# Router logits summed on VectorE from the output rows in some full slots of a two-layer mixture of experts

## The chip, the cores and the metric

The kernel runs on one core of one Trainium2 chip. The metric is the device time of one execution in microseconds (us). Before the change it is 702.29 us, the median of three runs (701.58 to 703.89).

## The reference, cut to what matters

A decayed linear attention (4 batches, 8 heads, 768 positions, head size 64) gives 3072 rows of 512. Two mixture-of-experts layers follow. The second layer's router reads the rows that the first layer gives out.

```python
def _moe_ref(x, modality_id, w_gate, modality_bias, w1, w2):     # layer 1
    logits = x @ w_gate + modality_bias[modality_id]
    e_idx = np.argmax(logits, axis=1)
    ...
    for e in range(E):
        h = np.maximum(x[mask] @ w1[e], 0.0)
        out[mask] = gate_w[mask, None] * (h @ w2[e])

def _moe2_ref(x, w_skip, w_gate, w1, w2):                        # layer 2
    skip_score = x @ w_skip
    do_compute = skip_score > 0
    xc = x[do_compute]
    logits = xc @ w_gate
    e_idx = np.argmax(logits, axis=1)
    ...
    out[do_compute] = xc + y
```

N = 3072 rows, D = 512, E = 8 experts, F = 1024, all fp32. For layer 2 every row of layer 1's output therefore needs nine dot products of length 512: eight columns of `w_gate` and one `w_skip`.

## The kernel before, in words

The attention comes first, and layer 1's router with it. It writes the rows to DRAM, and tables that tell which rows each expert gets. Then both layers work in **slots** of up to 256 rows of one expert. Layer 1 has up to 19 slots, layer 2 up to 20; how many there are, which expert each has, whether its weights are new and whether it has more than 128 rows (`full`) is computed on VectorE by `table` into the row of whole numbers `ei` (lines 208 to 278), and read into registers by `flag` (L318), `reg` (L315) and `is_full` (L324). All branches are taken at run time on these registers, on each engine by itself.

Matrix products are made in fp32r with a high and a low part of each operand, so each product is three matmuls. A full slot does this on TensorE, in this order (`slot`, from L850 on):

- `layer1` (L702): eight column tiles f of 128, twelve matmuls each, 256 columns moving, into the PSUM tiles `p1`. After each odd f ScalarE takes the high part `hh` (L718) and VectorE the low part `hl` (L719) of the hidden rows.
- `trans_x` (L347): eight transposes of the next slot's gathered rows `xg`; ScalarE copies the high part `xth`, VectorE takes the low part `xtl` (L355).
- `layer2` (L748) for rows 0 to 127 and then for rows 128 to 255: eight chunks of three matmuls, 512 columns moving. The third matmul of a chunk takes `hl`: chunks 0 to 3 those of f = 1 and 3, chunks 4 and 5 that of f = 5, chunks 6 and 7 that of f = 7. ScalarE scales the result into `x2r` (L762), which is stored to DRAM (`keep`) and scattered to the output.

A slot kk of layer 1 also carries layer 2's **router for the rows of slot kk-1** (`router`, L661), as steps between the column tiles:

```python
steps = {1: lambda: tr(kk - 1, ptr), 3: la, 4: rk}
```

`tr` (L668) transposes the 256 rows `x2r` on TensorE, eight transposes, and ScalarE copies them to `x2t` (L669); `la` (L675) makes the logits, sixteen matmuls of 32 rows into `plg`; `rk` transposes these on VectorE (L680) to `L` and makes mask, maximum, one-hot rows and counts (L682 to L685 and `route_a`, `route_s`, L115 to L133). `rb` then stands in `layer2` after chunk 3: two small matmuls of ranks (L137, L138), seven short operations on VectorE that end with the reciprocal (L158), and two scatters of the tables' rows on GpSimd.

Where a slot begins another expert, `split_w2` (L308) and `split_w1` (L302) split the new weights into high and low parts on ScalarE and VectorE. Slots that are not full take `layer1_half`. The order on each engine is the order of the code (a manual schedule); each engine waits on semaphores.

Of the kernel before, what the change touches and what calls it, by code (L numbers as in the profile page):

```python
# [9 lines left out]
F32 = mybir.dt.float32  # L10
# [8 lines left out]
P = 128  # L19
E = 8  # L20
# [14 lines left out]
@with_exitstack  # L35
def body(ctx: ExitStack, tc: tile.TileContext, qkv, cpk, w1, w2, out, dbg=None):
    nc = tc.nc
# [141 lines left out]
    def count(dst):  # L179
        n = rt.tile([P, E], F32, tag="t_n", name="t_n")  # L180
        nc.vector.tensor_tensor(out=n, in0=dst, in1=erow0, op=ALU.subtract)
        return n
# [5 lines left out]
    def choose(which, n):  # L188
        t = rt.tile([P, E], F32, tag="t_p", name="t_p")
        g = rt.tile([P, E], F32, tag="t_g", name="t_g")  # L190
        mx = rt.tile([P, 1], F32, tag="t_mx", name="t_mx")
        mp = rt.tile([P, 1], F32, tag="t_mp", name="t_mp")
# [12 lines left out]
        nc.vector.tensor_scalar(out=erow, in0=eid, scalar1=float(TP), scalar2=None, op0=ALU.mult)  # L205
        nc.vector.tensor_tensor(out=perm, in0=bc(eid.unsqueeze(2), [P, E, E]), in1=bc(ivec.unsqueeze(1), [P, E, E]), op=ALU.is_equal)

    def table(which):
        n = count(pcnt[which])
        x = rt.tile([P, KT, E], F32, tag="t_x", name="t_x")  # L210
        nr = rt.tile([P, E], F32, tag="t_nr", name="t_nr")
# [13 lines left out]
        nc.vector.tensor_copy(out=ei_[:, 4 * KT:4 * KT + 1], in_=cc[:, E:E + 1])  # L225
        ge = rt.tile([P, KT, E], F32, tag="t_ge", name="t_ge")
        nc.vector.tensor_tensor(out=ge, in0=bc(kvec.unsqueeze(2), [P, KT, E]), in1=bc(c1.unsqueeze(1), [P, KT, E]), op=ALU.is_ge)
        h = rt.tile([P, KT, E], F32, tag="t_h", name="t_h")
        nc.vector.tensor_tensor(out=h, in0=bc(kvec.unsqueeze(2), [P, KT, E]), in1=bc(cc[:, 0:E].unsqueeze(1), [P, KT, E]), op=ALU.is_ge)
# [5 lines left out]

        u = rt.tile([P, E], F32, tag="t_u", name="t_u")
        y = rt.tile([P, KT], F32, tag="t_y", name="t_y")
        base = rt.tile([P, KT], F32, tag="t_b", name="t_b")
        nc.vector.scalar_tensor_tensor(out=u, in0=cc[:, 0:E], scalar=-float(T), in1=erow, op0=ALU.mult, op1=ALU.add)
# [5 lines left out]
        pick(eid, y)  # L245
        nx = rt.tile([P, E, E], F32, tag="t_nx", name="t_nx")
        nc.vector.tensor_tensor(out=nx, in0=bc(c1.unsqueeze(2), [P, E, E]), in1=bc(c1.unsqueeze(1), [P, E, E]), op=ALU.is_ge)
        nxe = rt.tile([P, E], F32, tag="t_nxe", name="t_nxe")
        nc.vector.tensor_reduce(out=nxe, in_=nx, axis=AX.X, op=ALU.add)
        w = rt.tile([P, KT], F32, tag="t_w", name="t_w")  # L250
        hx = rt.tile([P, KT], F32, tag="t_hx", name="t_hx")
        g2 = rt.tile([P, E], F32, tag="t_g2", name="t_g2")
        g3 = rt.tile([P, E], F32, tag="t_g3", name="t_g3")
        nc.vector.tensor_scalar(out=g2, in0=nxe, scalar1=estar, scalar2=None, op0=ALU.add)
# [5 lines left out]
        fin = ge[:, :, E - 1]  # L260
        nw = rt.tile([P, KT - 1], F32, tag="t_nw", name="t_nw")
        if which:
# [10 lines left out]
        nc.vector.scalar_tensor_tensor(out=u, in0=cc[:, 0:E], scalar=float(T), in1=nr, op0=ALU.mult, op1=ALU.add)  # L273
        rem = rt.tile([P, KT], F32, tag="t_r", name="t_r")
# [48 lines left out]
    def is_full(ap):  # L323
        return nc.values_load(ap, engines=FE, min_val=0, max_val=1,  # L324
                              skip_runtime_bounds_check_because="it is a comparison's result")

# [335 lines left out]
    def router(ix, kk=None):  # L662
# [14 lines left out]

        def rk():
            L = rt.tile([P, 2, 32], F32, tag="L2", name="L2")
            nc.vector.transpose(out=L.rearrange("p j e -> p (j e)"), in_=plg)  # L680
            idf = rt.tile([P, 2], F32, tag="idf", name="idf")
# [19 lines left out]

        return tr, la, rk, rb  # L702

    def layer1(kk, steps):
        xh, xl = xth[kk % 2], xtl[kk % 2]
        for f in range(8):
            pt = p1[(f // 2) % 3]
# [14 lines left out]

    def layer1_half(kk, steps):
        fs_ = [steps[f] for f in sorted(steps)]
        xh, xl = xth[kk % 2], xtl[kk % 2]
        for g in range(2):
            o = p1[g].rearrange("p a t -> p (a t)")
            fs = slice(g * 512, (g + 1) * 512)
            for c in range(4):
                nc.tensor.matmul(o, xh[:, c, 0:P], w1h[c][:, fs], start=(c == 0), stop=False)  # L730
                nc.tensor.matmul(o, xl[:, c, 0:P], w1h[c][:, fs], start=False, stop=False)
                nc.tensor.matmul(o, xh[:, c, 0:P], w1l[c][:, fs], start=False, stop=(c == 3))
            nc.scalar.activation(out=hrow[g], in_=o.rearrange("p (a f) -> p a f", f=P), func=AF.Relu)
            if g < len(fs_):
                fs_[g]()
        for g in range(2):
# [4 lines left out]
            for a in range(2):  # L741
                as_ = slice(2 * a, 2 * a + 2)
                nc.vector.tensor_tensor(out=hl[g][:, as_, 0:P], in0=pt[:, as_], in1=f32(hh[g][:, as_, 0:P]), op=ALU.subtract)  # L743
        for st_ in fs_[2:]:
            st_()
# [31 lines left out]
    def first1():  # L777
# [26 lines left out]
        behind(ld_w1(e), got)  # L804
        ld_w2(e)
        gather_x(0, 2)
        fill()
# [5 lines left out]
    def first2():  # L813
        la, rk, rb = router(itl)[1:]

# [28 lines left out]
    def slots(which):  # L844
# [10 lines left out]
        def slot(kk, fl, full):  # L855
# [22 lines left out]
            if which == 0:  # L878
                tr, la, rk, rb = router(it[(kk - 1) % 6], kk - 1)
# [48 lines left out]

_INS = ["qkv", "cpk", "w1", "w2"]
_OUTS = [((3072, 512), "float32")]  # L930
# [50 lines left out]
```

## Time and profile before

| | |
|---|---|
| median of 3 runs (range) | 702.29 us (701.58 to 703.89) |
| profiled execution | 703.4 us |
| its span, first to last instruction | 701.7 us |
| busy: TensorE matmuls, weight loads | 671.0 us (96%), 596.9 us (85%) |
| busy: VectorE, ScalarE, GpSimd | 361.2 us (51%), 262.5 us (37%), 218.3 us (31%) |
| mean granted TensorE clock | 0.994 |
| moved by DMA | 109.67 MB, mean 156 GB/s |

The profile names engines PE (TensorE's matmuls), PEld (its weight loads), DVE (VectorE), ACT (ScalarE), POOL (GpSimd) and SP (the queue that issues most DMAs); a q behind the name means the engine's sequencer (register loads, branches, waits), which is not counted as busy. Busy times are shares of the whole span; attention, layer 1 and layer 2 follow one another in it, and what an engine's time is worth differs from one to the next. An engine's idle time costs nothing where another engine is the one waited for.

### The profile page before, as it was taken

The numbers are of one execution on the slowest core, as the hardware profiler recorded it, in microseconds if no ns is written. First come the engines' busy times: TensorE is split into PE (matmuls) and PEld (weight loads), VectorE is DVE, ScalarE is ACT, GpSimd is POOL, SyncE is SP. The second block draws the span as 40 slices with busy tenths as digits, with TensorE's granted clock in tenths as the row PEclk, the third lists the DMA queues.
The fourth block names the chain that finished last, engine by engine and source line by source line (L and its number), as shares of the span: only waits on it lengthen the run. The fifth ranks groups of instructions, "written<-read, shape, count | busy, mean of one in ns | idle before, by whom it ended". The sixth has DMA issues, their size and how long they took to land. (4 is left out here: it accounts for less than half of the span.)

```text
span 701.7 us, 16337 instructions
## 1 busy us (share of the span) xinstructions
PE 671.0 (96%) x5628; PEld 596.9 (85%) x5628; DVE 361.2 (51%) x924; ACT 262.5 (37%) x462; POOL 218.3 (31%) x287
## 2 busy tenths in 40 slices
PE   6999999899999999999999998988999999999993
PEld 5889988878988998789889987876998899887992
DVE  5656676763213315853133337858227575758650
ACT  2444434522221225822222227432116544556530
POOL 4356556343231132531311324323121112113121
PEclk9999999999999999999999999999999999999997
DMA  8778766747330133883201211722815558658500
GB/s 279 227 199 236 211 200 211 212 134 273 109 116 32 64 121 101 284 308 123 91 31 38 92 48 53 250 87 53 295 60 177 194 199 277 198 189 266 179 6 29
DMA packets 60505, 109.67 MB, mean 156 GB/s; under 512 B 18656, under 2 KB 18784, under 8 KB 60368
## 3 DMA queue, kind: packets, MB, share of 16 engines
q1 hardware_dynamic: 48400, 86.65, 38.4%
q0 software_dynamic: 9744, 20.47, 8.6%
q8 instruction: 61, 1.00, 0.6%
q10 hardware_dynamic: 2224, 0.93, 0.6%
q14 instruction: 76, 0.62, 0.3%
HBM read 84.08 MB, written 30.06 MB: 163 GB/s over the span
## 5 line engine op out<-in xcount | busy, mean ns | idle before, releaser
L711 PE MATMUL p<-xth,w1h 128*128 128x256 f32 x672 | 190.4, 283 | 6.3 <-ACTq L893 1.9
L712 PE MATMUL p<-xtl,w1h 128*128 128x256 f32 x672 | 187.3, 279 | 0.0
L713 PE MATMUL p<-xth,w1l 128*128 128x256 f32 x672 | 187.3, 279 | 0.0
L719 DVE SCALAR_TENSOR_TENSOR hl<-p,hh 128x512 fp32r<-128x512 f32 x84 | 57.7, 690 | 180.6 <-ACT hh L718 173.1
L752 PE MATMUL p<-w2h,hh 128*128 128x512 f32 x360 | 144.2, 401 | 0.0
L753 PE MATMUL p<-w2l,hh 128*128 128x512 f32 x360 | 141.3, 393 | 0.9 <-DVE w2l L312 0.8
L754 PE MATMUL p<-w2h,hl 128*128 128x512 f32 x360 | 141.5, 393 | 0.6 <-DVE hl L743 0.6
L711 PEld LDWEIGHTS p<-xth,w1h 128*128 128x128 f32 x672 | 126.2, 188 | 10.0 <-ACTq L893 2.4
L713 PEld LDWEIGHTS p<-xth,w1l 128*128 128x128 f32 x672 | 127.2, 189 | 0.1
L712 PEld LDWEIGHTS p<-xtl,w1h 128*128 128x128 f32 x672 | 126.4, 188 | 0.8 <-DVEq L772 0.2
L718 ACT ACTIVATE hh<-p 128x512 fp32r<-128x512 f32 x84 | 50.2, 598 | 183.4 <-PE p L713 181.0
L161 POOL DMA_INDIRECT out_dram<-x2r,it x43 | 46.5, 1081 | 204.1 <-DVE x2r L765 101.6
L754 PEld LDWEIGHTS p<-w2h,hl 128*128 128x128 f32 x360 | 67.6, 188 | 16.5 <-DVE hl L743 1.5
L753 PEld LDWEIGHTS p<-w2l,hh 128*128 128x128 f32 x360 | 67.7, 188 | 15.9 <-DVE w2l L312 2.6
L752 PEld LDWEIGHTS p<-w2h,hh 128*128 128x128 f32 x360 | 67.7, 188 | 13.1
L161 POOL DMA_INDIRECT tab<-pk,rows x28 | 31.9, 1140 | 143.4 <-issue 119.9
L165 POOL DMA_INDIRECT xg<-xs,it x54 | 60.1, 1112 | 30.8 <-issue 12.7
L312 DVE TENSOR_TENSOR w2l<-raw,w2h 128x1024 fp32r<-128x1024 f32 x48 | 55.9, 1219 | 7.6 <-ACT w2h L311 7.3
L311 ACT CAST w2h<-raw 128x1024 fp32r<-128x1024 f32 x48 | 49.1, 1048 | 23.6 <-issue 12.5
L762 ACT ACTIVATE x2r<-p,it 128x512 f32<-128x512 f32 x26 | 17.9, 688 | 106.8 <-PE p L754 97.1
L306 DVE TENSOR_TENSOR w1l<-raw,w1h 128x512 fp32r<-128x512 f32 x88 | 53.9, 682 | 0.8 <-ACT w1h L305 0.3
L305 ACT CAST w1h<-raw 128x512 fp32r<-128x512 f32 x88 | 47.0, 635 | 0.0
(215 smaller groups left out, 799.0 us busy)
## 6 DMA issues: line engine op xcount, KB each, us to landing
raw<-in_w_dram SPq DMA_DIRECT2D x96, 512.0 KB, 6.4
kq<-in_qkv_dram SPq DMA_DIRECT2D x48, 256.0 KB, 3.4
xs<-x2r SPq DMA_DIRECT2D x28, 256.0 KB, 2.6
v<-in_qkv_dram SPq DMA_DIRECT2D x24, 256.0 KB, 3.8
xs<-xr SPq DMA_DIRECT2D x24, 256.0 KB, 5.5
xs<-xgm SPq DMA_DIRECT2D x7, 512.0 KB
xg<-xs,it POOLq DMA_INDIRECT x54, 4.3
tab<-tini ACTq DMA_DIRECT2D x2, 416.0 KB
```

The costliest lines, as they stand in the source:

```text
L161: nc.gpsimd.indirect_dma_start(out=dst, out_offset=bass.IndirectOffsetOnAxis(ap=idx, axis=0), in_=rows, in_offset=None, bounds_check=dst.s ...
L165: return nc.gpsimd.indirect_dma_start(out=rows, out_offset=None, in_=src, in_offset=bass.IndirectOffsetOnAxis(ap=idx, axis=0), bounds_chec ...
L306: nc.vector.tensor_tensor(out=w1l[c][:, s], in0=raw1[:, c, s], in1=f32(w1h[c][:, s]), op=ALU.subtract)
L312: nc.vector.tensor_tensor(out=w2l[c], in0=r, in1=f32(w2h[c]), op=ALU.subtract)
L711: nc.tensor.matmul(o, w1h[c][:, fs], xh[:, c, :], start=(c == 0), stop=False)
L712: nc.tensor.matmul(o, w1h[c][:, fs], xl[:, c, :], start=False, stop=False)
L713: nc.tensor.matmul(o, w1l[c][:, fs], xh[:, c, :], start=False, stop=(c == 3))
L718: nc.scalar.activation(out=a, in_=pt, func=AF.Relu)
L719: nc.vector.scalar_tensor_tensor(out=b, in0=pt, scalar=0.0, in1=f32(a), op0=ALU.max, op1=ALU.subtract)
L752: nc.tensor.matmul(p2[j], a, w2h[g][:, i], start=(n == 0), stop=False)
L753: nc.tensor.matmul(p2[j], a, w2l[g][:, i], start=False, stop=False)
L754: nc.tensor.matmul(p2[j], b, w2h[g][:, i], start=False, stop=(n == 7))
```

## The change

A new input `wgr` holds the nine columns of the router's weights as nine rows of 512. One DMA in `first1` copies them to all 128 partitions (`wgb`). In slots 2 to 10 of layer 1 the logits of the preceding slot's rows can be computed on VectorE: for each of two halves of 128 rows and each of nine columns, one operation multiplies 512 elements of `x2r` with `wgb` and sums them into one element of `L` per partition (`lg`). `tr`, `la` and the VectorE transpose in `rk` are then left out.

Which slots do so is decided by the flag that said `full`. For layer 1 it now is 0 for up to 128 rows, 1 for a full slot, and 2 for a full slot whose predecessor and successor have the same expert. The slot's first layer is cut in three parts with a branch each: f = 0 and 1; f = 2 and 3 with the router, in three arms (flag 2: `lg`; flag 1: as before; flag 0: half); f = 4 to 7. Temporaries of `table`, `choose` and `rk` get one buffer each in place of two.

```diff
+    wgb = hp.tile([P, E + 1, D], F32, name="wgb")
...
-        nc.vector.tensor_scalar(out=ei_[:, 3 * KT:4 * KT], in0=rem, scalar1=float(P), scalar2=None, op0=ALU.is_gt)
+        if which:
+            nc.vector.tensor_scalar(out=ei_[:, 3 * KT:4 * KT], in0=rem, scalar1=float(P), scalar2=None, op0=ALU.is_gt)
+        else:
+            nc.vector.tensor_tensor(out=w[:, 0:KT - 2], in0=nw[:, 0:KT - 2], in1=nw[:, 1:KT - 1], op=ALU.max)
+            nc.vector.tensor_scalar(out=w[:, 0:KT - 2], in0=w[:, 0:KT - 2], scalar1=-1.0, scalar2=2.0, op0=ALU.mult, op1=ALU.add)
+            nc.vector.scalar_tensor_tensor(out=ei_[:, 3 * KT + 1:4 * KT - 1], in0=rem[:, 1:KT - 1], scalar=float(P),
+                                           in1=w[:, 0:KT - 2], op0=ALU.is_gt, op1=ALU.mult)
...
+        def lg(j, es):
+            for e in es:
+                nc.vector.tensor_tensor_reduce(
+                    out=x2t[:, :, j], in0=x2r[kk % 2][j].rearrange("p (c t) -> p c t", t=P),
+                    in1=wgb[:, e].rearrange("p (c t) -> p c t", t=P), scale=1.0, scalar=0.0, op0=ALU.mult, op1=ALU.add,
+                    accum_out=box["L"][:, j, e:e + 1])
...
         ld_w2(e)
+        nc.sync.dma_start(out=wgb, in_=bc(wgr.unsqueeze(0), [P, E + 1, D]))
         gather_x(0, 2)
...
-            with tc.If(full > 0, preferred_fallthrough_block=True) as c:
-                layer1(kk, steps)
-            with c.Else():
-                layer1_half(kk, {} if which else {1: steps[1], 3: lambda: (la(), rk())})
+            if which == 0 and 2 <= kk <= 10:
+                box["L"] = rt.tile([P, 2, 32], F32, tag="L2", name="L2", bufs=1)
+                own = nc.values_load(ei[0][0:1, 3 * KT + kk:3 * KT + kk + 1], engines=(ET.DVE,), min_val=0, max_val=2,
...
+                with tc.If(own > 1):
+                    lg(0, range(E + 1))
+                with tc.If(full > 0, preferred_fallthrough_block=True) as c:
+                    layer1(kk, {}, (0, 1))
+                with c.Else():
+                    half_rows(kk, 0)
+                with tc.If(full > 1, preferred_fallthrough_block=True) as c:
+                    lg(1, range(0, 4))
+                    layer1(kk, {}, (2, 3))
+                    lg(1, range(4, E + 1))
+                    rk(True)
+                with c.Else():
+                    with tc.If(full > 0, preferred_fallthrough_block=True) as c2:
+                        steps[1]()
+                        layer1(kk, {}, (2, 3))
+                        la()
+                        rk()
+                    with c2.Else():
+                        steps[1]()
+                        half_rows(kk, 1)
+                        la()
+                        rk()
+                with tc.If(full > 0, preferred_fallthrough_block=True) as c:
+                    layer1(kk, {}, range(4, 8))
+                with c.Else():
+                    half_cols()
+            else:
...
```

`layer1_half` is cut into `half_rows` and `half_cols` with the same operations; the other slots keep the old code.

The change moves instructions at three places.

TensorE, slot 2, from the last matmul of f = 1 to the first of f = 2. `ptr` are the PSUM tiles of the transposes, `p_1876` and `p_1879` those of f = 0, 1 and f = 2, 3. Before:

```order
L713 MATMUL p_1876<-xth_164,w1l_145 128x256
L668 MATMUL ptr_1877<-ident,x2r_1872 128x128 [waits Activation_49]
L668 MATMUL ptr_1877<-ident,x2r_1872 128x128 x3
L668 MATMUL ptr_1878<-ident,x2r_1873 128x128 [waits Activation_49,Pool_49]
L668 MATMUL ptr_1878<-ident,x2r_1873 128x128 x3
L711 MATMUL p_1879<-xth_164,w1h_138 128x256
```

Now (the first two rows are the end of the arm for slots that are not full, which the branch L918 follows):

```order
L747 MATMUL p_1877<-w1l_145,xth_164 128x512 [waits DVE_49]
L914 UNCONDITIONAL_BRANCH
L918 COMPARE_AND_BRANCH
L728 MATMUL p_1880<-xth_164,w1h_138 128x256
L729 MATMUL p_1880<-xtl_166,w1h_138 128x256
L730 MATMUL p_1880<-xth_164,w1l_142 128x256
```

The transposes stand in front of f = 2 no longer, and neither do the logits' products in front of f = 4; a branch stands there.

VectorE, slot 2, from the register loads on. Before (`hl` is the hidden rows' low part, `pmi` the PSUM tile of the logits):

```order
L318 TENSOR_LOAD ei_168
L324 TENSOR_LOAD ei_168
L884 COMPARE_AND_BRANCH
L719 SCALAR_TENSOR_TENSOR hl_1866<-p_1876,hh_1864 128x512 [waits Activation_49]
L719 SCALAR_TENSOR_TENSOR hl_1866<-p_1879,hh_1864 128x512 [waits Activation_49]
L680 STREAM_TRANSPOSE L_2881<-pmi 128x64 [waits PE_49]
L682 CAST idf<-it_159 128x2 [waits DMAHW4_49]
```

Now:

```order
L324 TENSOR_LOAD ei_168
L330 TENSOR_LOAD ei_168
L910 TENSOR_LOAD ei_168
L912 COMPARE_AND_BRANCH
L687 ISA x2t,L_2794<-x2r_1872,wgb 128x4x128 [waits DMAHW7_49,Activation_49]
L687 ISA L_2794 128x1
L687 ISA x2t,L_2794<-x2r_1872,wgb 128x4x128 [waits DVE_49]
```

Each sum is two instructions, the sum and the readout of its result. Nine such pairs stand ahead of `hl` of f = 1, four between `hl` of f = 1 and of f = 3, five between `hl` of f = 3 and the ranking, which `hl` of f = 5 follows. Each sum after the first waits for the readout in front of it.

SP, in `first1`, behind the loads of the second expert's weights (`raw`). Now:

```order
L296 DMA raw_137<-in_w_dram 128x2x512 [waits DMAHW6_49,DVE_49]
L829 DMA wgb<-in_wgr_dram 128x4608 [waits DMAHW7_49,PE_49,Pool_49]
L792 DMA xs_63<-x2r_1870 128x512 [waits DMAHW0_49,Activation_49]
L324 TENSOR_LOAD ei_168
L795 COMPARE_AND_BRANCH
```

The copy of the table stands between the weights and the first store of rows; before, that store came directly behind the weights.

## Rows read from the trace of the kernel before

**Rows 1.** The page, busy us (share of the span) and instructions of each engine.

```profile
PE 671.0 (96%) x5628; PEld 596.9 (85%) x5628; DVE 361.2 (51%) x924; ACT 262.5 (37%) x462; POOL 218.3 (31%) x287
```

**Rows 2.** Stretches: length, busy us of each engine (instructions), granted clock, DMA share, GB/s.

```profile
202.90:227.62 24.72, 24.72 (x195) 22.32 (x194) 6.83 (x26) 5.81 (x11) 6.44 (x9) 1.00 0.25 84
...
561.02:583.80 22.78, 22.78 (x153) 20.80 (x152) 14.63 (x20) 11.72 (x18) 4.41 (x4) 1.00 0.65 219
```

**Rows 3.** Timeline of PE, slot 3: start, us, engine, line, operation, tiles, shape, count.

```profile
205.52 0.28 PE L713 MATMUL p<-xth,w1l 128*128 128x256 f32 x1
205.64 1.04 PE L668 MATMUL ptr<-ident,x2r 128*128 128x128 f32 x8
...
210.24 0.28 PE L712 MATMUL p<-xtl,w1h 128*128 128x256 f32 x1
```

**Rows 4.** Timeline of PE, later in the same slot.

```profile
215.47 0.28 PE L713 MATMUL p<-xth,w1l 128*128 128x256 f32 x1
215.58 1.04 PE L351 MATMUL ptr<-ident,xg 128*128 128x128 f32 x8
...
219.22 0.18 PE L137 MATMUL pmi<-oh,tri 128*128 128x16 bf16 x1
...
219.83 0.39 PE L754 MATMUL p<-w2h,hl 128*128 128x512 f32 x1
...
227.39 0.40 PE L754 MATMUL p<-w2h,hl 128*128 128x512 f32 x1
227.62 0.28 PE L711 MATMUL p<-xth,w1h 128*128 128x256 f32 x1
```

**Rows 5.** Timeline of DVE, the same slot; in brackets idle time before, and who ended it.

```profile
206.52 0.69 DVE L719 SCALAR_TENSOR_TENSOR hl<-p,hh 128x512 fp32r<-128x512 f32 x1 [10.58 <-ACT hh L718]
...
210.94 0.13 DVE L682 CAST idf<-it 128x2 f32<-128x2 int32 x1
...
212.41 0.17 DVE L127 TENSOR_TENSOR oh<-oh,mk 128x16 bf16<-128x16 bf16 x1
212.62 0.36 DVE L133 TENSOR_TENSOR rs<-rs,oh 128x8 bf16<-128x8 bf16 x2
...
216.41 0.69 DVE L719 SCALAR_TENSOR_TENSOR hl<-p,hh 128x512 fp32r<-128x512 f32 x1 [1.97 <-ACT hh L718]
217.02 1.27 DVE L355 TENSOR_TENSOR xtl<-ptr,xth 128x512 fp32r<-128x512 f32 x2
219.46 0.17 DVE L141 COPY rs<-rs 128x8 bf16<-128x8 bf16 x1 [1.16 <-PE pmi L138]
...
220.56 0.17 DVE L158 RECIPROCAL pk<-s 128x2 f32<-128x2 f32 x1
```

**Rows 6.** Timeline of ACT, the same slot: the first half of the output rows.

```profile
222.32 0.69 ACT L762 ACTIVATE x2r<-p,it 128x512 f32<-128x512 f32 x1 [4.87 <-PE p L754]
```

**Rows 7.** DVE: a timeline row of eight; then groups by form, busy us, mean ns.

```profile
270.33 4.91 DVE L306 TENSOR_TENSOR w1l<-raw,w1h 128x512 fp32r<-128x512 f32 x8
...
L122 DVE SCALAR_TENSOR_TENSOR sc<-dd,pri 128x16 f32<-128x16 f32 x14 | 2.5, 175 | 0.5
L685 DVE SCALAR_TENSOR_TENSOR mk<-L,pres 128x2 f32<-128x2 f32 x14 | 2.3, 161 | 0.5
L233 DVE TENSOR_TENSOR t_x<-t_h,t_nxe 128x192 f32<-128x192 f32 x2 | 0.7, 358 | 0.1
L234 DVE TENSOR_REDUCE t_w<-t_x 128x24 f32<-128x192 f32 x2 | 0.7, 352 | 0.1
L198 DVE TENSOR_SCALAR eb<-estar 128x1 int32<-128x1 f32 x4 | 0.6, 154 | 0.1
```

**Rows 8.** DVE's sequencer, 220 to 223: ns min/median/max, first and last start.

```profile
L324 DVEq TENSOR_LOAD <-ei x1: 304/304/304, 222.2 to 222.2; - x1
...
L884 DVEq COMPARE_BRANCH  x1: 50/50/50, 222.6 to 222.6; - x1
```

**Rows 9.** DMA from 150 to 175 in 40 slices of 0.625 us, all queues.

```profile
GB/s 249 157 164 203 118 249 354 354 321 367 308 203 269 374 413 419 400 400 406 400 393 387 390 387 380 413 393 416 423 384 226 107 47 0 0 0 0 2 1 324
```

More of the change, by code (lines that the diff above doesn't have):

```diff
@@ L35, in body @@
 @with_exitstack
-def body(ctx: ExitStack, tc: tile.TileContext, qkv, cpk, w1, w2, out, dbg=None):
+def body(ctx: ExitStack, tc: tile.TileContext, qkv, cpk, w1, w2, wgr, out, dbg=None):
     nc = tc.nc
@@ L188, in choose @@
     def choose(which, n):
[L189 to L192, printed above, removed]
+        t = rt.tile([P, E], F32, tag="t_p", name="t_p", bufs=1)
+        g = rt.tile([P, E], F32, tag="t_g", name="t_g", bufs=1)
+        mx = rt.tile([P, 1], F32, tag="t_mx", name="t_mx", bufs=1)
+        mp = rt.tile([P, 1], F32, tag="t_mp", name="t_mp", bufs=1)
         b = eb[:, which]
@@ L245, in table @@
         pick(eid, y)
-        nx = rt.tile([P, E, E], F32, tag="t_nx", name="t_nx")
+        nx = rt.tile([P, E, E], F32, tag="t_nx", name="t_nx", bufs=1)
         nc.vector.tensor_tensor(out=nx, in0=bc(c1.unsqueeze(2), [P, E, E]), in1=bc(c1.unsqueeze(1), [P, E, E]), op=ALU.is_ge)
-        nxe = rt.tile([P, E], F32, tag="t_nxe", name="t_nxe")
+        nxe = rt.tile([P, E], F32, tag="t_nxe", name="t_nxe", bufs=1)
         nc.vector.tensor_reduce(out=nxe, in_=nx, axis=AX.X, op=ALU.add)
[L250 to L253, printed above, removed]
+        w = rt.tile([P, KT], F32, tag="t_w", name="t_w", bufs=1)
+        hx = rt.tile([P, KT], F32, tag="t_hx", name="t_hx", bufs=1)
+        g2 = rt.tile([P, E], F32, tag="t_g2", name="t_g2", bufs=1)
+        g3 = rt.tile([P, E], F32, tag="t_g3", name="t_g3", bufs=1)
         nc.vector.tensor_scalar(out=g2, in0=nxe, scalar1=estar, scalar2=None, op0=ALU.add)
@@ L260, in table @@
         fin = ge[:, :, E - 1]
-        nw = rt.tile([P, KT - 1], F32, tag="t_nw", name="t_nw")
+        nw = rt.tile([P, KT - 1], F32, tag="t_nw", name="t_nw", bufs=1)
         if which:
@@ L323, in is_full @@
     def is_full(ap):
-        return nc.values_load(ap, engines=FE, min_val=0, max_val=1,
-                              skip_runtime_bounds_check_because="it is a comparison's result")
+        return nc.values_load(ap, engines=FE, min_val=0, max_val=2,
+                              skip_runtime_bounds_check_because="it comes from comparisons' results")
     def XG(which, kk):
@@ L676, in la, with rk @@
                                      start=(c == 0), stop=(c == 3))
-        def rk():
-            L = rt.tile([P, 2, 32], F32, tag="L2", name="L2")
-            nc.vector.transpose(out=L.rearrange("p j e -> p (j e)"), in_=plg)
+        def lg(j, es):
[4 more added lines that the diff above has]
+                    accum_out=box["L"][:, j, e:e + 1])
+        def rk(have=False):
+            L = box.get("L")
+            if L is None:
+                L = rt.tile([P, 2, 32], F32, tag="L2", name="L2", bufs=1)
+            if not have:
+                nc.vector.transpose(out=L.rearrange("p j e -> p (j e)"), in_=plg)
             idf = rt.tile([P, 2], F32, tag="idf", name="idf")
@@ L700, in rb, with layer1 @@
                 scatter(tabv[1][j], pk[:, j, :], rows[:, j:j + 1])
-        return tr, la, rk, rb
-    def layer1(kk, steps):
+        return tr, la, rk, rb, lg
+    def layer1(kk, steps, fr=range(8)):
         xh, xl = xth[kk % 2], xtl[kk % 2]
-        for f in range(8):
+        for f in fr:
             pt = p1[(f // 2) % 3]
@@ L721, in layer1, with half_rows, half_cols @@
                 steps[f]()
-    def layer1_half(kk, steps):
-        fs_ = [steps[f] for f in sorted(steps)]
+    def half_rows(kk, g):
         xh, xl = xth[kk % 2], xtl[kk % 2]
[L726 to L735, printed above, removed]
+        o = p1[g].rearrange("p a t -> p (a t)")
+        fs = slice(g * 512, (g + 1) * 512)
+        for c in range(4):
+            nc.tensor.matmul(o, xh[:, c, 0:P], w1h[c][:, fs], start=(c == 0), stop=False)
+            nc.tensor.matmul(o, xl[:, c, 0:P], w1h[c][:, fs], start=False, stop=False)
+            nc.tensor.matmul(o, xh[:, c, 0:P], w1l[c][:, fs], start=False, stop=(c == 3))
+        nc.scalar.activation(out=hrow[g], in_=o.rearrange("p (a f) -> p a f", f=P), func=AF.Relu)
+    def half_cols():
         for g in range(2):
@@ L743, in layer1_half @@
                 nc.vector.tensor_tensor(out=hl[g][:, as_, 0:P], in0=pt[:, as_], in1=f32(hh[g][:, as_, 0:P]), op=ALU.subtract)
+    def layer1_half(kk, steps):
+        fs_ = [steps[f] for f in sorted(steps)]
+        for g in range(2):
+            half_rows(kk, g)
+            if g < len(fs_):
+                fs_[g]()
+        half_cols()
         for st_ in fs_[2:]:
@@ L813, in first2 @@
     def first2():
-        la, rk, rb = router(itl)[1:]
+        la, rk, rb = router(itl)[1:4]
         def arm(l1, js):
@@ L878, in slot @@
             if which == 0:
-                tr, la, rk, rb = router(it[(kk - 1) % 6], kk - 1)
+                tr, la, rk, rb, lg = router(it[(kk - 1) % 6], kk - 1)
                 steps = {1: lambda: tr(kk - 1, ptr), 3: la, 4: rk}
@@ L882, in slot @@
             full2 = is_full(ei[which][0:1, 3 * KT + kk + 1:3 * KT + kk + 2])
-            with tc.If(full > 0, preferred_fallthrough_block=True) as c:
-                layer1(kk, steps)
-            with c.Else():
-                layer1_half(kk, {} if which else {1: steps[1], 3: lambda: (la(), rk())})
+            if which == 0 and 2 <= kk <= 10:
+                box["L"] = rt.tile([P, 2, 32], F32, tag="L2", name="L2", bufs=1)
+                own = nc.values_load(ei[0][0:1, 3 * KT + kk:3 * KT + kk + 1], engines=(ET.DVE,), min_val=0, max_val=2,
+                                     skip_runtime_bounds_check_because="it comes from comparisons' results")
+                with tc.If(own > 1):
[23 more added lines that the diff above has]
+                with c.Else():
+                    half_cols()
+            else:
+                with tc.If(full > 0, preferred_fallthrough_block=True) as c:
+                    layer1(kk, steps)
+                with c.Else():
+                    layer1_half(kk, {} if which else {1: steps[1], 3: lambda: (la(), rk())})
+            box.pop("L", None)
             trans_x(which, kk + 1, ptr)
@@ L926, in body @@
         dbg(nc, locals())
-_INS = ["qkv", "cpk", "w1", "w2"]
+_INS = ["qkv", "cpk", "w1", "w2", "wgr"]
 _OUTS = [((3072, 512), "float32")]
@@ L963 @@
         _np.ascontiguousarray(ids).view(_np.float32)], axis=1)
+    inputs["wgr"] = _np.concatenate([_np.asarray(inputs[n]).reshape(hd, -1) for n in ("moe2_w_gate", "moe2_w_skip")], axis=1).T
     inputs["w1"] = _np.concatenate([inputs["moe_w1"], inputs["moe2_w1"]], axis=0)
```

24 lines of the change are left out of this document (12 added, 12 removed).

## The prediction

> **What bounds the kernel now.** I read the page's busy times first, then a table of stretches, then the timelines of one slot, engine by engine. TensorE is busy for 96% of the span [rows 1], so a change pays by what it takes out of TensorE's stream, unless it makes TensorE wait. The slot from 202.90 to 227.62 is a full slot of layer 1 with the router in it. [...]
>
> **Where it acts.** The reference's inputs send 1494, 6, 1319 and 253 rows to four experts in layer 1, which makes slots 0 to 5, 6, 7 to 12 and 13; 6 and 12 have 128 rows or fewer. The flag is 2 where the slots on both sides have the same expert, and the new code stands in slots 2 to 10 alone: it runs in 2, 3, 4, 8, 9 and 10. Slots 5, 6 and 7 keep the old steps in the other arms. So: six slots, in two runs of three.
>
> **What it removes.** In the slot shown, the last matmul of f=1 starts at 205.52 and the second of f=4 at 210.24: 4.72 us for 26 steps of the stream, with eight transposes between [rows 3] and the logits' products. From 210.24 to the last of f=7 at 215.47 there are 46 steps in 5.23 us [rows 3, 4], 0.114 us each. Without the router the 26 steps take 2.96 us: **1.76 us saved a slot, 10.6 us in six.** [...] The slot would be 24.72 - 1.76 = 22.96 us. Two ScalarE copies a slot go too; nobody waits for them but the removed products.
>
> **What it adds on VectorE.** Eighteen sums a slot, each a product of 128x512 fp32 with a running sum, and behind each a readout of one element; the next sum waits for that readout. No row shows the pair, so I build its pitch p. Eight subtractions of 128x512 fp32, both inputs in SBUF, with no wait between them take 4.91 us [rows 7]; with 0.69 for the last, a step is (4.91 - 0.69)/7 = 0.60. Reducing costs nothing extra: 192 elements take 352 ns reduced, 358 multiplied [rows 7]. A one-element operation takes 154 ns [rows 7]. From an end to the start of an operation that waits for it is 0.04 us (212.41 + 0.17, then 212.62 [rows 5]). **p = 0.60 + 0.15 + 0.04 = 0.79.** Below, 0.73: only the write of the sum counts (0.69 + 0.04). Above, 0.92: the readout starts only when the sum is written (0.69 + 0.04 + 0.15 + 0.04). I take 0.79, because independent operations do overlap by 0.09 in that row and the readout waits on nothing.
>
> [...]
>
> **Does VectorE keep up?** Times from the slot's start. The first nine sums need the first half of the last slot's rows, written at 222.32 + 0.69, which is 4.61 before the next start at 227.62 [rows 4, 6]. Nine sums are 7.1 us, so they end at 2.5, before hl of f=1 at h = 206.52 - 202.90 = 3.62 [rows 5]. Then come two hl at a step of 0.61 (216.41 to 217.02), nine sums, the ranking (210.94 to 212.62 + 0.36: 2.04) and hl of f=5 (0.69). That hl is written at h + 1.22 + 9p + 2.73. TensorE needs it at 219.83 - 202.90 - 1.76 = 15.17, less about 0.1 for the wait [rows 4, 5]: **no stall while h + 9p is at most 11.1**; with p = 0.79 that means h up to 4.0. The rank products need the ranking's one-hot rows at 219.22 - 202.90 - 1.76 = 14.56 and have them earlier.
>
> VectorE's own cycle: 18p, four hl (2.44), the ranking (2.04), two xtl (1.2), 220.56 - 219.46 = 1.10 for the rows' places, and from there to the slot's branch at 222.6 another 2.04, to which the third register load adds 0.30 [rows 5, 8]. Together 18p + 9.13 = **23.35 us against TensorE's 22.96**: each slot of a run starts its hl 0.39 later than the one before, until TensorE waits. In the run 8 to 10, h is 3.62, 4.0, 4.4: stalls of 0, 0 and 0.4.
>
> **The table.** The copies of the router's weights are 128 x 18 KB = 2.36 MB, queued on SP behind 4.2 MB of weights. That queue's load keeps the DMA near 390 GB/s until slice 31 of 40 in 150 to 175, about 169.4 [rows 9]; 2.36 MB more at that rate is 6.0 us, to 175.4. Slot 2 starts at 178.17 and would begin its sums at 173.6; begun at 175.4 they end at 4.4 instead of 2.5. So h is 4.4 and the first run stalls about 0.4 in each slot: 1.3. What queues behind the table (one store of rows, the index rows for slot 4) is needed only after 180.
>
> **What costs nothing.** The added branches on TensorE: at 227.62 it has passed two and a slot's end at its usual step of 0.23 [rows 4]; if that cover went, each would cost some tenths. Two more short operations in the slot table (0.4) lie under a wait for gathered rows. Single buffers for temporaries that VectorE alone uses add no wait.
>
> **Sum.** The profiled execution took 703.4 (span 701.7). 703.4 - 10.6 + 1.3 + 0.4 = 694.5. It was 1.1 above the median of the runs, 702.29; from that: **693.4 us**.
>
> **Rivals.**
> 1. *VectorE becomes the bound* (slower). If the readout follows the written sum, p is 0.88 to 0.92, the cycle 25.0 to 25.7, and TensorE waits 2.0 to 2.7 us a slot for hl of f=5: 702 to 706. It decides at p = 0.88, where cycle and old slot meet. For it: there is under 0.1 us of room in p, and each 0.01 is worth 1 us. Against it: the overlap in rows 7. Chance 0.22, of which 0.14 is slower and 0.08 the same.
> 2. *Half rate* (much slower). If the sum moves one element in two cycles, a sum takes 0.53 us more, p = 1.32: 18 x 1.32 + 9.13 = 32.9 us a slot. The four later slots take 8.2 us more each than now, the first of each run about 7: near 749. Against it: two-input operations on fp32 in SBUF take 161 ns for 2 elements and 175 for 16 [rows 7], one nanosecond an element, full rate; but these have no sum. [...] Chance 0.07.
> 3. *The arm is not taken or only partly pays*: flag 2 never read, all as before, 702.3 (chance 0.03, same); or the table lands 4 us later, or arms further apart make TensorE wait for code, and 3 to 6 us of the gain go: 697 to 699.5 (chance 0.08, faster).
>
> **How the numbers follow.** The forecast has 0.60: p up to 0.83, 691.7 (no stall at all) to 697.5, likeliest 693.4. A measurement can tell 0.3% (2.1 us) from no change. Faster: 0.60 + 0.08 = 0.68. Same: 0.08 + 0.03 = 0.11. Slower: 0.14 + 0.07 = 0.21. For 8 in 10 the range takes in the forecast, the partial gains and most of rival 1, from 691.0 (the floor less a spread between runs) to 705.3; the half rate and the worst of rival 1 stay out. The forecast's own range is 691 to 697.5.
>
> **What would show it.** Right: in the six slots no transposes of x2r and no products, f=1 to f=4 at a step of 1.36 us, a slot of 23.0 to 23.4 us, sums at a pitch near 0.79. Wrong: a pitch of 0.88 or more with TensorE idle before the third matmul of chunk 4, released by hl; or slots still at 24.7; or VectorE in slot 2 waiting past 176 for the table.

## The result, and the profile after

The changed kernel takes 712.33 us (median of six runs) against 702.21 for the kernel before in the same series: a ratio of 1.013, 95% interval 1.0104 to 1.0156. It is slower, by about 9 us by the ratio, where 9 us faster was forecast. One of the six runs (720.7 us) is over 1.5% above the fastest and is left out of the ratio. The profiled execution took 712.63 us (span 710.9, mean granted clock 0.983 against 0.994).

The page, the same rows as [rows 1], then the groups of layer 2's third matmul and of the sums (busy us, mean ns of one, idle time before and who ended it):

```profile
PE 665.6 (94%) x5388; PEld 589.2 (83%) x5388; DVE 434.2 (61%) x1136; ACT 256.7 (36%) x450; POOL 222.4 (31%) x287
...
L777 PE MATMUL p<-w2h,hl 128*128 128x512 f32 x360 | 144.4, 401 | 12.1 <-DVE hl L736 11.2
...
L687 DVE CUSTOM_DVE_ANT_0 x2t<-x2r,wgb 128x512 f32<-128x512 f32 x108 | 74.8, 692 | 20.2 <-ACT x2r L785 13.1 <-DMA wgb<-in_wgr_dram 3.9
```

There are 108 sums, 18 in each of six slots, as forecast, and TensorE runs 240 matmuls less. But it now stands for 11.2 us in front of layer 2's third matmul (L777), behind the hidden rows' low part. In the kernel before, no wait for `hl` in a full slot of layer 1 could be seen [rows 4].

Stretches of after: slot 3, a part of it, and slot 7 (length, busy us of PE, PEld, DVE, ACT, POOL, granted clock, DMA share, GB/s):

```profile
200.63:227.35 26.72, 24.92 (x155) 21.75 (x154) 19.14 (x62) 4.85 (x9) 6.88 (x9) 0.94 0.22 78
216.10:219.70 3.60, 3.60 (x12) 2.53 (x11) 1.54 (x9) 0.00 (x0) 0.00 (x0) 0.53 0.02 5
295.16:323.57 28.41, 26.52 (x194) 24.04 (x195) 18.50 (x48) 8.93 (x14) 10.45 (x11) 0.94 0.72 230
```

Slot 3 lasts 26.72 us against 24.72 in [rows 2]. TensorE's timeline in it, to be held against [rows 4]:

```profile
212.65 0.40 PE L776 MATMUL p<-w2l,hh 128*128 128x512 f32 x1
214.84 0.50 PE L777 MATMUL p<-w2h,hl 128*128 128x512 f32 x1 [1.80 <-DVE hl L736]
215.18 0.39 PE L775 MATMUL p<-w2h,hh 128*128 128x512 f32 x1
...
216.77 0.63 PE L775 MATMUL p<-w2h,hh 128*128 128x512 f32 x1
```

This L777 belongs to **chunk 0**, whose data is the `hl` of f = 1. Yet TensorE waits 1.80 us for an `hl` of VectorE that ends at 214.78. Soon after the wait the matmuls take 0.63 us in place of 0.39: from 216.1 to 219.7 the granted clock is 0.53. VectorE's timeline in the same slot, to be held against [rows 5]:

```profile
204.25 0.69 DVE L736 SCALAR_TENSOR_TENSOR hl<-p,hh 128x512 fp32r<-128x512 f32 x1 [1.52 <-ACT hh L735]
204.86 0.68 DVE L687 CUSTOM_DVE_ANT_0 x2t<-x2r,wgb 128x512 f32<-128x512 f32 x1
205.47 0.09 DVE L687 DVE_READ_ACCUMULATOR2_ANT L<- 128x1 f32 x1
205.59 0.69 DVE L687 CUSTOM_DVE_ANT_0 x2t<-x2r,wgb 128x512 f32<-128x512 f32 x1
...
211.82 0.16 DVE L699 CAST idf<-it 128x2 f32<-128x2 int32 x1
...
214.09 1.29 DVE L736 SCALAR_TENSOR_TENSOR hl<-p,hh 128x512 fp32r<-128x512 f32 x2 [0.20 <-issue]
```

The `hl` of f = 1 was written at 204.94, ten microseconds before chunk 0 ran. What ends at 214.78 is the first of two at 214.09: the `hl` of **f = 5**, behind nine sums and the ranking.

Where the time of the two profiled executions went (stretches of both traces):

| | before | after | |
|---|---|---|---|
| slots 2 to 4 and 8 to 10 | 148.42 | 155.45 | +7.0 |
| slots 5 and 6 | 40.75 | 42.75 | +2.0 |
| slot 7 | 24.90 | 28.41 | +3.5 |
| start of slot 2 | 178.17 | 175.59 | -2.6 |
| the rest | | | -0.7 |
| span | 701.7 | 710.9 | +9.2 |

The start of slot 2 lies between 175.6 and 181.3 in this run and those below; nothing is read from that row. In the six slots 11.2 us are the waits. Slots 3, 8 and 10 last 1.6 us longer than slots 2 and 4 with the same wait (granted clock 0.94 in each of the three, 1.00 in the two): 4.8 us of lower clock. With the forecast saving of 10.6 us that makes +5.4; the other 1.6 us of the +7.0 I have not put down to rows.

### The profile page after: what moved, and what is told of

Same layout as the page of the kernel before. It is cut to its first block, busy times and chain, and to the rows that moved or that the text cites. A ratio compares the mean times of both kernels' runs of the same rounds, so it can differ in the third digit from the quotient of the medians.

```text
span 710.9 us, 16316 instructions
## 1 busy us (share of the span) xinstructions
PE 665.6 (94%) x5388; PEld 589.2 (83%) x5388; DVE 434.2 (61%) x1136; ACT 256.7 (36%) x450; POOL 222.4 (31%) x287
## 5 line engine op out<-in xcount | busy, mean ns | idle before, releaser
L777 PE MATMUL p<-w2h,hl 128*128 128x512 f32 x360 | 144.4, 401 | 12.1 <-DVE hl L736 11.2
L775 PE MATMUL p<-w2h,hh 128*128 128x512 f32 x360 | 146.0, 406 | 0.0
L776 PE MATMUL p<-w2l,hh 128*128 128x512 f32 x360 | 142.8, 397 | 1.1 <-DVE w2l L318 1.0
L161 POOL DMA_INDIRECT out_dram<-x2r,it x43 | 49.1, 1142 | 202.2 <-DVE x2r L788 100.2
L777 PEld LDWEIGHTS p<-w2h,hl 128*128 128x128 f32 x360 | 68.6, 191 | 30.9 <-DVE hl L736 14.1
L687 DVE CUSTOM_DVE_ANT_0 x2t<-x2r,wgb 128x512 f32<-128x512 f32 x108 | 74.8, 692 | 20.2 <-ACT x2r L785 13.1
L312 DVE TENSOR_TENSOR w1l<-raw,w1h 128x512 fp32r<-128x512 f32 x88 | 53.9, 684 | 0.8 <-ACT w1h L311 0.3
```

The lines of the kernel that those rows point to most:

```text
L161: nc.gpsimd.indirect_dma_start(out=dst, out_offset=bass.IndirectOffsetOnAxis(ap=idx, axis=0), in_=rows, in_offset=None, bounds_check=dst.s ...
L312: nc.vector.tensor_tensor(out=w1l[c][:, s], in0=raw1[:, c, s], in1=f32(w1h[c][:, s]), op=ALU.subtract)
L687: nc.vector.tensor_tensor_reduce(out=x2t[:, :, j], in0=x2r[kk % 2][j].rearrange("p (c t) -> p c t", t=P), in1=wgb[:, e].rearrange("p (c t) ...
L775: nc.tensor.matmul(p2[j], a, w2h[g][:, i], start=(n == 0), stop=False)
L776: nc.tensor.matmul(p2[j], a, w2l[g][:, i], start=False, stop=False)
L777: nc.tensor.matmul(p2[j], b, w2h[g][:, i], start=False, stop=(n == 7))
```

## What TensorE waits for

In the built program each engine counts its finished operations in a semaphore, and others wait for a value of that count. All arms of a branch raise it by the same total (to 353 in branch 2 of slot 2, to 357 in branch 3), and the code behind the branch waits for one number whichever arm ran. The numbers of slot 2 (VectorE's count after each step; branch 2 holds f = 2, 3 and the router, branch 3 f = 4 to 7; columns are the half arm's hidden rows, which `half_cols` transposes and splits):

```
                     summing arms                    half arms
branch 2   333-336 four sums, 337 hl f=3,    342 logits transposed
           338-342 five sums,
           343-353 ranking                   343-353 ranking
branch 3   356 hl f=5 (adds 3), 357 hl f=7   354, 355 columns 0-3; 356, 357 columns 4-7
wait of chunk 0: 354   of chunk 2: 355   of chunk 4: 356   of chunk 6: 357
```

In the half arm 354 is chunk 0's `hl`. In the summing arm the first operation that reaches 354 is `hl` of f = 5. In the kernel before one branch held all of the layer, and chunk 0 waited for the last operation but one of the ranking, which was written by 212.98 [rows 5], 3.9 us ahead of chunk 0's third matmul at 216.92; it cost nothing and could not be seen.

**Theory J** is that this number makes the stall. **Rival V**: VectorE is late by itself. **Rival B**: the added branches cost the time. For slots 5 to 7, **theory S**: the sums' scratch `x2t` is also the logits' operand, and slots that take no sums still wait for VectorE to come past the branch around them. In slot 7 of after, all waits, then ScalarE's timeline:

```profile
ACT x2t L676 <- DVEq L912: 2.8, 1, 2.8
...
PE pmi L682 <- ACT x2t L676: 1.9, 1, 1.9
```

```profile
302.62 1.07 ACT L676 COPY x2t<-ptr 128x512 f32<-128x512 f32 x2 [2.76 <-DVEq L912]
```

L912 is the branch around the first nine sums. VectorE's sequencer reaches it, not taken, behind a burst of weight splits; ScalarE's copy waits 2.76 us for that, TensorE 1.9 us for the copy.

## The experiments

Three series; the kernel before took 707.36, 703.03 and 702.6 us in them, so each run is read by its ratio to before.

**e1_cols_first** moves the half arm's columns ahead of its ranking, and so their places in the count:

```diff
-                        la()
-                        rk()
+                        la()
+                        half_cols()
+                        rk()
...
-                with c.Else():
-                    half_cols()
```

> The change as it is, but in the arm for half slots the hidden rows' columns (half_cols) stand ahead of the ranking and inside the second branch; the third branch holds f=4 to f=7 alone. A full slot runs the same instructions in the same order as in the changed kernel; only the place that the half arm's low parts have in VectorE's count differs. Theory J (joined count): behind the branches TensorE waits for one value of VectorE's count, whichever arm ran, and in the changed kernel the value for chunk 0 is one that the summing arm reaches only with hl of f=5. Then the six stalls of 1.8 us ahead of chunk 0's third matmul (11.2 us) go, with them the stretches of lower granted clock in slots 3, 8 and 10 (about 1.6 us each), and the time is 712.3 - 11.2 - 4.8 = about 696; slots 5 to 7 stay as they are (slot 7: 28.4 us). Rival V (VectorE is late by itself): the wait only moves to chunk 4, which needs hl of f=5, and the time stays at 708 to 712. Rival B (the branches cost the time): unchanged, 712.

Measured: 741.84 us, ratio 1.0481 (1.0444 to 1.0519). The time went the wrong way by 30 us, and none of the three was right about it. The stall at chunk 0 did go. In its place stood this one at the head of f = 4 (TensorE, then VectorE, slot 3):

```profile
217.65 0.55 PE L728 MATMUL p<-xth,w1h 128*128 128x256 f32 x1 [4.04 <-DVE L L687]
```

```profile
217.42 0.08 DVE L687 DVE_READ_ACCUMULATOR2_ANT L<- 128x1 f32 x1
```

f = 4 has no business with a sum. But the half arm's columns pass through the PSUM tile `p1` that f = 4 writes, and their readers now stand in branch 2: f = 4 waits for value 339, in the summing arm the second sum behind `hl` of f = 3. That is theory J's mechanism at a place that I had not looked at; all six slots have it (22.3 us in waits).

**e4_both** is e1 with the scratch of e2.

> Both edits: half columns ahead of the ranking, and the sums' products into hrow1. By J and S together no stall is left: six slots of 23.0 us, slot 7 near 24.9, slots 5 and 6 near 41, granted clock 0.99: 712.3 - 16 - 5 = about 691.5, the sum that was forecast. Rival V: hl of f=5 is late for chunk 4, 700 to 707. Rival B: 705 or more, since all the branches are still there.

Measured: 742.37 us, 1.0467 (1.0412 to 1.0523), for e1's reason: six waits at f = 4, 23.2 us. It tells nothing more.

**e2_scratch:**

```diff
-                    out=x2t[:, :, j], in0=...
+                    out=hrow[1], in0=...
```

> The change with one edit: the sums' products, which nobody reads, go to hrow1 in place of x2t. Theory S (shared scratch): in slots 6 and 7, whose sums are not taken, ScalarE's copies into x2t wait until VectorE has come past the branch around the sums, behind its splits of weights, and the logits' products wait for the copies. Then the waits of 1.3 and 1.9 us ahead of those products go, and the stretch of lower clock behind the second one: slot 7 falls from 28.4 to about 24.9 us, slots 5 and 6 together from 42.8 to about 41.4, the time from 712.3 to about 707. The six stalls at chunk 0 stay at 1.8. Rival B (the extra branches and register loads themselves): slot 7 stays near 28.4 and the time at 712.

Measured: 717.56 us, 1.0159 (1.0099 to 1.0219), no faster than the changed kernel (1.013) where 5 us were expected. Slot 7 fell to 25.03 us, as S says, and its copies wait no more. But slots 5 and 6 rose to 44.8: the half slot 6 writes `hrow1` itself, ScalarE waited 0.6 us there for the same branch, and TensorE 2.5 us for the ranking ahead of the half columns. The price moved from slot 7 to slot 6. The six stalls stayed.

**e3_one_branch:**

```diff
+                with tc.If(full > 1, preferred_fallthrough_block=True) as c:
+                    lg(0, range(E + 1))
+                    layer1(kk, {1: lambda: lg(1, range(0, 4)), 3: lambda: (lg(1, range(4, E + 1)), rk(True))})
+                with c.Else():
+                    with tc.If(full > 0, preferred_fallthrough_block=True) as c2:
+                        layer1(kk, steps)
+                    with c2.Else():
+                        layer1_half(kk, {1: steps[1], 3: lambda: (la(), rk())})
```

> The sums with one branch a slot as before the change, but three arms that each hold the whole first layer: sums; transposes and products; half. The nine sums of the first half stand at the head of their arm. The half arm keeps its old order, ranking before columns. Theory J: the cut is not what costs; the value for chunk 0 is now the last operation but one of the ranking, some 0.9 us ahead of the end of hl of f=5, so the stall at chunk 0's third matmul shrinks from 1.8 to about 0.9 us in each of the six slots and does not go. Theory S: there is no branch around the sums any more, so slots 5 to 7 lose their waits (5 us). Together 699 to 704, by how often the clock falls. Rival B (cuts and branches cost it): no stall is left, 691 to 694.

Measured: 706.86 us, 0.9989 (0.9963 to 1.0015). In slots 3 and 4 the wait at chunk 0 has the size that J worked out from the count, 0.81 us for 0.9, and its releaser is the ranking, L133. In slots 2, 8, 9 and 10 another wait came first, ahead of the next slot's transposes. TensorE's timeline in slots 3 and 8, then a DMA window of 0.2 us within slot 8 (8 is the queue of instructions):

```profile
217.26 0.50 PE L777 MATMUL p<-w2h,hl 128*128 128x512 f32 x1 [0.81 <-DVE rs L133]
...
336.39 0.41 PE L357 MATMUL ptr<-ident,xg 128*128 128x128 f32 x2 [1.40 <-ACT hh L735]
```

```profile
DMA  0000000000000900000000000000000000000000
...
q8 instruction: 1, 0.02, 33.9%
```

The value of ScalarE's count that L357 asks for in the program was reached with the `hh` of f = 1, 8.8 us before, so that is not what it waits for. One 16 KB packet of instructions began at 333.77, and TensorE went on 2.6 us later. L357 is the first matmul behind the arm's end, where TensorE jumps over two more arms that hold the whole layer each. I call this **theory C**: the stop is code. What S expected did not come: slots 5 to 7 last 71.8 us together, as long as in the changed kernel (71.2; before 65.6), with other waits (1.9 and 1.4 us for the largest in slots 6 and 7), which were not followed up.

**e9_clear** is the version that J asks for, e1 with the half columns in another PSUM tile, and the scratch of e2:

```diff
-            pt = (p1[2], p1[0])[g].rearrange("p a (b t) -> p (a b) t", b=2)
+            pt = p2[g].rearrange("p (b t) -> p b t", t=P)
...
-                    out=x2t[:, :, j], in0=...
+                    out=hrow[1], in0=...
```

> The changed kernel with the places in the count cleared: half columns ahead of the ranking (as in e1), but transposed into layer 2's own PSUM tiles p2, so that f=4 of a full slot no longer waits for a value that stands among the sums; and the sums' products into hrow1. By theory J the last values that TensorE waits for in a summing slot are now the fourth of the five sums behind hl of f=3 for chunk 0 (due some 3 us before it), and hl of f=5 for chunk 4: no stall in the six slots, 23.0 us each against 24.7 before the change, slot 7 near 25.0, slots 5 and 6 together 41 to 43 against 40.8. So 10.6 less 0.3 to 2.3 below the kernel before: 8 to 10 us faster, granted clock 0.99. Rival V (VectorE is late by itself): a stall ahead of chunk 4, slots near 24.7, the time within 2 us of before. Rival B (branches and cuts cost it): slower than before.

Measured: **692.0 us, ratio 0.9856 (0.9826 to 0.9887)**: by the ratios 10 us faster than before, and 19 us faster than the changed kernel with the same sums. Its two runs of three slots, then TensorE and VectorE in slot 3:

```profile
176.30:245.35 69.05, 69.05 (x463) 62.49 (x462) 52.63 (x173) 14.55 (x27) 21.70 (x27) 1.00 0.25 85
311.07:379.95 68.88, 68.88 (x464) 62.14 (x463) 52.26 (x171) 14.55 (x27) 21.74 (x27) 1.00 0.22 73
```

```profile
211.47 0.39 PE L776 MATMUL p<-w2l,hh 128*128 128x512 f32 x1
211.70 0.39 PE L777 MATMUL p<-w2h,hl 128*128 128x512 f32 x1
```

```profile
212.86 1.29 DVE L736 SCALAR_TENSOR_TENSOR hl<-p,hh 128x512 fp32r<-128x512 f32 x2
```

Chunk 0 runs at 211.70, and the `hl` of f = 5 starts at 212.86: it never needed it. In the program chunk 0 now asks for value 339, the second sum behind `hl` of f = 3. Six slots take 137.93 us, 10.5 less than before, with TensorE busy throughout; slot 7 takes 24.94, slots 5 and 6 40.78. V and B fall: the sums and the three branches are all still there.

**e8_cols_p2** is e9 without the new scratch.

> As e9_clear, but the products stay in x2t. J: the six slots at 23.0 us. S: slot 7 is back at about 28 us and slot 6 waits for the copies of x2t, so the time is 3 to 5 us above e9_clear. If S is wrong, the same as e9_clear.

Measured: 698.07 us, 0.9945 (0.9915 to 0.9974). The six slots take 23 us each, slot 7 29.3 with 2.7 us of TensorE behind the copies of `x2t`. S is worth 6 us once J's stall is gone, a little over the 3 to 5 expected.

**e6_one_ahead:**

```diff
                     lg(0, range(E + 1))
+                    lg(1, range(0, 1))
...
-                    lg(1, range(0, 4))
+                    lg(1, range(1, 4))
```

> The change with one of the nine sums of the second half moved from behind hl of f=1 to ahead of it, where VectorE is idle for about a microsecond. Nothing else moves. J: hl of f=5 comes one pitch, 0.735 us, sooner, and the stall at chunk 0 shrinks from 1.8 to 1.1 us in each of the six slots: 4.4 us less than the changed kernel, and more if the clock then falls less often. Rival B: no change.

Measured: 708.51 us, 1.0078 (1.0048 to 1.0109). Slots 3 and 4 wait 1.13 and 1.15 us and last 24.4 instead of 26.7 and 25.1; in slot 2 the table lands later and holds the sums up (the first begins at 174.91, 2.6 us ahead of the slot, for 3.0), the wait is 1.96 us and the slot 26.8. Slots 8 to 10 wait 1.14, 1.35 and 1.15 us, against 1.86, 2.10 and 1.82. One pitch of sums (0.73) is about one pitch of stall (0.67 to 0.75).

**e5_arms_only** keeps the branches with the old steps in the arm of flag 2:

```diff
-                    lg(1, range(0, 4))
+                    steps[1]()
                     layer1(kk, {}, (2, 3))
-                    lg(1, range(4, E + 1))
-                    rk(True)
+                    la()
+                    rk()
```

> The branches alone: the slot's first layer cut in three with three arms, flag, table's copy and single buffers as in the change, but the arm for flag 2 holds the old transposes, products and ranking; no sums and no branch around them. J: TensorE still waits for hl of f=5 at chunk 0, but that is written about 2.5 us ahead of it where no sums stand in front; so no stall, slots of 24.7 to 24.9 us, within 2 us of the kernel before. Rival B: the six slots are slower by 1 us and more, 6 to 10 us above before.

Measured: 713.67 us, 1.0141 (1.0112 to 1.0171), a miss for J as stated, and by its size B's number. But B says that every slot pays, and four of the six last 24.8 to 25.0. Slots 3 and 8 last 29.0 and 28.7. TensorE in slot 3, then a DMA window from 211.5 to 211.7:

```profile
211.52 0.28 PE L728 MATMUL p<-xth,w1h 128*128 128x256 f32 x1
214.27 0.37 PE L729 MATMUL p<-xtl,w1h 128*128 128x256 f32 x1 [2.48 <-issue]
```

```profile
DMA  0000200000000000000090000000010000000000
...
q8 instruction: 1, 0.02, 36.7%
```

TensorE stops in the middle of a column tile, four matmuls behind the end of branch 2, waiting for nothing that the profile shows, and the packet begins at 211.60. In slot 8 it stops at the first matmul behind branch 2. In 214.27 to 218.60 the granted clock is 0.62.

**e10_cuts_only** takes the third arm away again (old steps, `If(full > 0)` with two arms in branch 2).

> The cuts alone, without more code: the first layer of a slot in three branches as in the change, but two arms each (full, half) with the old steps; the flag, the table's copy and the single buffers stay, no sums. In e5_arms_only TensorE stood for 2.5 and 2.2 us in slots 3 and 8 waiting for nothing that the profile shows, and each time one 16 KB packet of the instruction queue began within 0.1 us of the stop. Theory C (code): the added arm with its transposes and products, which TensorE has to jump over or fetch, moved the program so that these fetches came too late; without it they go, and with them the lower clock behind them: six slots of 24.7 to 25.0 us, the time within 3 us of the kernel before. Rival B (each cut costs by itself): still 8 to 11 us above before.

Measured: 705.38 us, 1.0039 (1.0019 to 1.0058). No stop in any of the six slots, which last 24.7 to 25.0:

```profile
204.32:229.06 24.74, 24.74 (x195) 22.32 (x194) 6.93 (x26) 5.81 (x11) 6.44 (x9) 1.00 0.26 84
```

A cut by itself costs next to nothing (0.3 us in the six slots together); 2.8 us are left by the medians, in the profiled execution slots 5 to 7 are 1.4 us longer, and the cause stays open. Slots 3 and 8 of e5 are 4.2 and 3.9 us longer than here: the old steps in a third arm cost 8 us there, by the two stops (2.48 and 2.2 us) and the lower clock behind them (0.94 in each of the two slots).

**e7_one_cols** is e3 with `layer1_half(kk, {1: steps[1], 3: la, 4: rk})`, columns ahead of the ranking.

> As e3_one_branch, with the half arm's columns ahead of the ranking. J: the wait for the ranking at chunk 0 (0.8 us in slots 3 and 4) goes, these slots fall from 24.05 to 23.0 us. C: TensorE's waits of 1.3 to 1.4 us ahead of the next slot's transposes in slots 2, 8, 9 and 10, each 2.5 to 2.6 us behind the start of an instruction packet, have nothing to do with VectorE and stay, or move to other slots if the code shifts: these slots 24.4. Together about 1.7 us less than e3_one_branch, 1 to 4 us under before. If the waits of 1.4 us came from the join too, they go as well and the time is 8 us under before.

Measured: 700.3 us, 0.9962 (0.9944 to 0.9979). Slots 3 and 4 last 22.94 us, their waits are gone; slots 2, 8, 9 and 10 keep theirs (waits of TensorE between 170 and 420):

```profile
PE ptr L357 <- ACT hh L735: 5.8, 4, 1.6
```

So two different things stood in e3, one of VectorE's count and one of code. In the six slots of e3, e5 and e7 all ten stops end 2.5 to 2.9 us after the start of an instruction packet. That the jump is the cause is argued from this and from e10, and not shown; a kernel with only its code moved was not tried. A jump and a packet are not enough for a stop: in slots 3 and 4 of e3 and e7 TensorE takes the same jump, a packet begins 0.1 to 0.5 us ahead of it (214.50 in slot 3 of e3, L357 at 214.95), and L357 follows at once. Nine of the ten stops stand at the first matmul behind the jump; the tenth, in slot 3 of e5, stands four matmuls further.

**e11_two_more** is e9 with column 0 summed twice in each half, 20 sums a slot.

> e9_clear with one sum more in each half (column 0 is summed twice), 20 sums a slot in place of 18. With the measured pitch 0.735 VectorE's own cycle by the prediction's sum is 18 x 0.735 + 9.13 = 22.36 us, 0.6 under TensorE's 22.95; with 20 sums it is 23.83, 0.9 over. If that sum is right, the first slot of each run of three starts its sums in time, the later ones fall behind until TensorE waits for hl of f=5 at chunk 4: stalls of 0, about 0.7 and 0.9 us, 3 us above e9_clear. If VectorE has more room than the sum says: no change. If the cycle counts from the first slot on: 5 us.

Measured: 699.49 us, 0.9953 (0.9938 to 0.9968), 7 us above e9, where 3 were expected for the likeliest and 5 if the cycle counts from the first slot on. Waits from 170 to 420:

```profile
PE p L777 <- DVE hl L736: 2.1, 5, 0.6
```

They stand at chunk 4, where the prediction had put the need. The slots last 24.0, 24.0, 24.5 and 23.2, 23.7, 24.2 us, against 23.83 for VectorE's cycle by the prediction's sum. Of the 5.7 us that the six slots last longer than in e9, 2.1 show as waits for `hl` and 3.1 as longer busy time of TensorE at a granted clock of 1.00, which was not followed up. VectorE's room in e9 is under two sums a slot: V is not what happened, but it is near.

## Why the prediction was wrong

**The step that failed** is "TensorE needs it at 219.83 - 202.90 - 1.76 = 15.17": the need of `hl` of f = 5 was taken from the data, at chunk 4. The program asks for it at chunk 0, which would have run at 212.65 + 0.23 = 212.88, 12.25 us into slot 3. Everything else in that sum was good: with the measured pitch, h + 1.22 + 9p + 2.73 = 3.62 + 1.22 + 6.60 + 2.73 = 14.17, and `hl` of f = 5 was written at 214.78 - 200.63 = 14.15. Held against 12.25 the same formula gives a stall of 1.9 us; 1.8 was measured. So the mechanism that failed is the wait: which value of VectorE's count stands behind the branches.

- **The saving**, 1.76 us a slot and 10.6 in six: e9 shows 10.5. In after it is in the slots too, f = 1 to 4 step by 1.36 us, under the stalls.
- **The pitch**, 0.79 forecast, is 0.73, the lower bound: three pitches take 2.20 us (sums start at 209.00 and at 211.20). The sum's own part is 0.62 to the start of its readout, where 0.60 stood; the readout was mis-sized, 0.082 for 0.15; the step to the next sum is 0.03. That the lower bound was met is chance: it left the readout out, and the readout is there but short. The readout starts 0.07 us before the sum's row ends (0.692).
- **Rival 2, half rate**, is refuted: a sum takes 692 ns for 512 elements, a subtraction of that shape with both inputs in SBUF (L312, as L306 in [rows 7]) 684. The 0.53 us more that half rate was to cost is about what 512 elements take over two (0.69 in [rows 5], 0.16 in [rows 7]); the sum takes 0.008 us more than the subtraction.
- **Rival 1** named the right queue (`hl` of f = 5 behind the sums), a price close to the measured one (2.0 to 2.7 us a slot), and the wrong place and condition: it wanted p of 0.88 (by its own sum cycle and old slot meet at 0.87), and the stall came at 0.73.
- **The table**, 1.3 us, and VectorE's cycle, 0.4 us: nothing. The first sum waited 3.9 us for it and began at 172.57, 3.0 ahead of slot 2, where 2.8 was forecast; with the shorter pitch the nine sums end as `hl` of f = 1 comes due. With that pitch the cycle is 22.3 us, under TensorE's 22.96.
- **"What costs nothing"** failed twice. Slots 5 to 7 "keep the old steps", but not for free: 5.5 us, by the shared scratch and by lower clock behind the waits (0.94 in slot 7). And the branches' cover on TensorE was sought in their own time, 0.23 us a step, where what counts is which number stands behind them and, as far as e5 and e10 show it, how much code.

The range ended at 705.3 and missed. The case "slower" was in it, at 0.21, by mechanisms that did not act.

## What to carry to other kernels

Behind a branch, an engine of these kernels waits for a count that all arms share: for each wait behind the place where the arms meet, find the operation that reaches the number in the arm that runs, not the one that writes the data. Work moved to an engine "with room" delays whatever stands behind it in that count (here `hl` of f = 5, and by it chunk 0, for 1.80 to 2.10 us a slot), so put the operations that all arms owe the code behind that place ahead of the long ones, and give arms no tiles in common that the taken path doesn't need. Arms that repeat long code can cost nearly what they save (8 us in e5, against 10.5 saved in e9), here by stops that end 2.5 to 2.9 us behind the start of a packet of instructions; that the jump makes them is argued.

## What was unexpected in the hardware

- The stops put down to code end 2.5 to 2.9 us behind the start of a 16 KB packet of instructions (ten cases); TensorE stood for 1.2 to 2.5 us of it.
- Three of the six waits at chunk 0 in the changed kernel, in slots 3, 8 and 10 (1.80, 1.86 and 1.82 us), were followed by a stretch of lower granted clock (0.94 over each of these slots), at about 1.6 us extra each; the others, in slots 2, 4 and 9 (1.81, 1.84 and 2.10 us), were not (1.00). The granted clock was 0.94 too over the slots with the waits behind the copies of `x2t` in slot 7 (1.9 us in the changed kernel, 2.7 in e8), the two stops of e5 (2.48 and 2.2 us) and the wait in slot 2 of e6 (1.96 us). It was 1.00 in slots 2 and 8 to 10 of e3 and e7 and in slots 3, 4 and 8 to 10 of e6, with waits of 1.1 to 1.6 us. The length of the wait alone does not decide it: the longest of the six, 2.10 us in slot 9, is among those without.
- The readout of a running sum starts 0.07 us before the sum's own row ends (0.62 us after the sum's start, against 0.692 for the sum).
